# Attention beside a gated MLP on one core: shifted keys by SBUF copies, zero products in TensorE's pauses

## Chip, core and metric

The kernel runs on one core of a Trainium2 chip. The metric is the device time of one launch in microseconds (us), lower is better. The engines are named as in the profile: PE is TensorE (matrix products; PEld is its weight load), ACT is ScalarE, DVE is VectorE, POOL is GpSimd, SP is SyncE, which here only issues DMAs.

## What is computed

Two blocks read the same x (2048 rows, 512 columns), and a sigmoid gate mixes their outputs row by row. Block A is attention with 32 query heads of width 16 over one shared key and value head. Block B is a gated MLP whose gate goes through a 2048 x 2048 product along the sequence.

```python
# S = 2048, D = 512, H = 32, Dh = 16, Fh = 688; bfloat16
g = sigmoid((x * gate_w).sum(-1, keepdims=True))
q = (x @ wq).reshape(S, H, Dh);  k = x @ wk;  v = x @ wv        # one key/value head
p = softmax(q_h @ k.T * Dh ** -0.5);  a = concat_h(p @ v) @ wo
z = gelu(x @ w_in);  z1, z2 = z[:, :Fh], layernorm(z[:, Fh:])
b = (z1 * (w_sp @ z2 + b_sp[:, None])) @ w_out
out = g * a + (1 - g) * b
```

## The kernel before

All data stay in SBUF. The queries, keys and values lie transposed, with heads along partitions. x is loaded by four transposing DMAs, one for each chunk of 512 rows; the chunks come in the order `XO = (0, 3, 2, 1)`.

**Units and blocks.** Attention runs in `NU = 32` units. Unit u takes chunk u // 8 of the queries and four heads. Its scores are 64 blocks: 16 key tiles of 128 rows (`NKT`), times four heads `g` that lie in four partition groups of 32. A block is a product of 32 partitions, 128 keys x 512 queries (`s_mm`, name ps<-QA,KA). The blocks of a unit go two ways. Most are read from PSUM by ACT, which takes the exponential (`exp_op`, P<-ps, two or three blocks in one instruction). The others, up to `NMAX = 8` batches of four blocks a unit, are approximated by a polynomial on DVE: a linear step out of PSUM (`d_A`, UW<-ps), a square (`d_u`) and a second square (`d_w`, UW<-UW), of which POOL takes a part. PE then multiplies all results with the values (ps<-P,V; ps<-UW,V; ps<-UW,VW) and adds two closing products per unit (ps<-QA,KTV and ps<-CT,SVB), whose operands POOL prepares in the head. A unit's products with the values begin when those of the unit before are through.

**Two halves of the keys.** A head has 16 values, a partition group 32. One query tile `QA` thus holds two units: unit 2i uses the lower 16 partitions of each group, unit 2i + 1 the upper 16. `KA[:, 0, :]` holds the keys in the lower halves with zeros above, `KA[:, 1, :]` the shifted keys, in the upper halves with zeros below. Each is a product of x with a weight tile that has zero columns in the other half: `wk_r[0]` is `wk_rep`, `wk_r[1]` lies in the last 512 columns of `z1f` (names xT,wk_rep and xT,z). `g_K(c, lo, hi, e)` makes the products of a chunk, four pieces of four products, and DVE casts them out of PSUM (L426, KA<-ps).

**The planner.** The order of the instructions is planned when the kernel is built. `pe_step`, `act_step` and `dve_step` simulate PE, ACT and DVE with constant durations; each takes the next ready work when it is free, and the instructions are emitted into each engine's queue in that order. On the chip a queue runs strictly in order and waits on semaphores, whatever the plan thought. Constants steer the choice: `A_OV` is the overhead of one ACT instruction in ns, `FLEX` the backlog of DVE (ns) under which the PSUM bank 4, which both can use, goes to DVE instead of to a third block for ACT, `N0 = 3` the batches that unit 0 may give to DVE. `T[key]` is the planned time at which something is ready; the weights `win` have a constant there, 28000 ns. At most `ND = 5` batches are open at once, and a batch of unit u needs the last chunk of that unit's keys (`("K1", 3)` for an odd unit).

**The head.** `WARM` products of constants run before the first x is there. The list `first` holds, in order, the keys, first queries and values of the four chunks, then the shifted keys of the four chunks. Where PE finds no work and was busy for less than `W_MIN` (0.9) of the last `W_WIN` (3400 ns), `pe_step` emits a zero product (ps<-CT,zer, four products into a free bank), but only after 20 us of planned time.

**SP's queue** holds the x transposes, a query weight load, then `ld_win` and `ld_rest` (the bias row, `wo` in eight DMAs, `wout`, the first transposed `w_sp`). These later loads are chained: each waits until the one before has landed (`sp_dma`).

**The end.** After the last unit DVE normalises, and four products each finish the last four tiles of 128 rows (`g_out(14)`, `g_out(15)`, `g_fin(12)`, `g_fin(13)`). Tiles 14 and 15 leave PSUM through ACT (`outsb<-ps,G`), the former is stored by SP's queue, the latter by ACT's.

Of the kernel before, what the change touches and what calls it, by code (L numbers as in the profile page):

```python
# [7 lines left out]
ALU = mybir.AluOpType  # L8
# [8 lines left out]
DH = 16  # L17
# [4 lines left out]
NU = 32  # L22
# [18 lines left out]
NZ = 22  # L41
WARM = 12
RLAST = 16
XO = (0, 3, 2, 1)
N0 = 3
A_OV = 63.3
HEAD = 45000.0
# [8 lines left out]
W_GEL = 0.98  # L56
PR = dict(HALF=100.0, IDR=10, IDN=4, WRES=16, D_HG=2500.0, D_FL=False, WIN=1000.0, WIH=560.0, BACK=32, PRESS=5, FLEX=5000.0, RMIN=32, WBL=0.5, W_MIN=0.9, HOLD=0.0, RLEND=0)
SCHED = {}
# [108 lines left out]
def build_kernel(nc, x_d, wq_d, wk_d, wv_d, wo_d, win_d, wsp_d, bsp_d, wout_d, gw_d, out_d):  # L167
    es = ExitStack()
    with es:
# [75 lines left out]
        SF = tmp[:, 64 * NMAX:96 * NMAX].rearrange("p (k w) -> p k w", w=32)  # L245
        wk_r = [wk_rep[:], z1f[:, 512 * NZ - 512:512 * NZ].rearrange("p (a n) -> p a n", a=4)]
        PT = z2[:, 0:2048].bitcast(F32).rearrange("p (a n) -> p a n", a=2)
# [6 lines left out]
        op("dve", lambda v: v.memset(CT[:], 1.0 / 64.0), w=["CT"])  # L254
# [39 lines left out]
        op("act", lambda q: q.dma_start(wvg[:, :, 0:DH], wv_d.rearrange("(dt p) d -> p dt d", p=128)), w=["wv"], dma=16)  # L294
        op("act", nonc(lambda q: q.dma_start(wvg[:, :, 2 * DH:2 * DH + 1], gw_d.rearrange("(dt p one) -> p dt one", p=128, one=1))), w=["gw"], dma=16)
        def ld_win():
            sp_dma(lambda q: q.dma_start(win[:], win_d.rearrange("(dt p) n -> p dt n", p=128)), w=["win"])
# [28 lines left out]
        for e in range(2):  # L326
            op("dve", lambda v, e=e: v.tensor_scalar(wk_r[e].rearrange("p a (g e d) -> p a g e d", e=2, d=DH)[:, :, :, e, :],
                                                     wk_sb[:].unsqueeze(2).broadcast_to([128, 4, 4, DH]), 0.25, None, ALU.mult),
               r=["wk"], w=[("wk_rep", e)])

# [30 lines left out]

        ld_win()
        ld_rest()
        for _ in range(WARM):
# [53 lines left out]

        def g_K(c, lo=0, hi=512, e=0, b=BM):
            key = "K0a" if c == XO[0] and lo == 0 and e == 0 else ("K%d" % e, c)  # L420

            def piece(dt):
                return lambda: fm(b, hi - lo, 0, wk_r[e][:, dt, :], xT[:, dt, 512 * c + lo:512 * c + hi], dt == 0, dt == 3, [("wk_rep", e), ("x", c), ("z1", 5)], "K")

            def ev():
                op("dve", lambda v: v.tensor_copy(KA[:, e, 512 * c + lo:512 * c + hi], bank(b, hi - lo)), r=[bkey(b)], w=[key], tag="Kev")  # L426
# [469 lines left out]
        for i, c in enumerate(XO):  # L896
# [240 lines left out]
        def pv_emit(pu, rnd, t_end):  # L1137
            for g, it in rnd:
                pv_items[pu][g].remove(it)
                pv_done[pu] += 1  # L1140
                pv_g[pu][g] += 1
                it[1](st_["ua"] > pu and pv_g[pu][g] == unit_total(pu) // 4)
                if it[3] is not None:
                    kind, ix = it[3]
                    if kind == "P":
                        pbusy_[ix] = False
                        pfree_[ix] = t_end + 250.0
                    else:
# [87 lines left out]
        pbusy = deque()  # L1236
        pidle = [0]

        def pe_step(now):
            r = pe_work(now)  # L1240
            if r is None:
# [470 lines left out]
        if INFO is not None:  # L1712
            print({"end": last_end, "busy": busy, "batches": len(batches), "hist": hist, "left": left, "sbuf": nc.sbuf_bytes_remaining})
            print("warm", pidle[0])
            INFO.update(T=T, units=units, estart=estart, stepb=stepb, busy=busy, log=log)
        if INFO is not None and st_["pu"] < NU:
# [177 lines left out]
```

## Time and profile before

| | us |
|---|---|
| three runs, median | 729.7 |
| lowest and highest | 729.62 and 729.8 |
| profiled execution, device time | 732.05 |
| its span, first to last instruction | 730.2 |

In the profile a row of a group gives the line, the engine, the operation, the output and inputs by the program's names, the shape and the count, then the busy time and the mean duration, then the idle time just before and what ended it. A row of a timeline gives the start in us, the length in us, the engine, line and names, and in brackets the idle time before. A row of windows gives each engine's busy time in a stretch and at its end the granted PE clock as a share of full speed, the DMA engines' busy share and GB/s. A row of one tile's instructions gives the shortest, median and longest duration in ns and the first and last start in us. DMA rows give the size of one and the median time from issue to landing.

### The profile page before, as it was taken

What the parts mean: (1) busy time and instruction counts of PE and PEld (TensorE: products, weight loads), DVE (VectorE), ACT (ScalarE), POOL (GpSimd) and SP (SyncE); (2) the same over time, 40 slices, a digit from 0 to 9 for tenths busy, and PEclk for the clock granted to TensorE, in tenths of its full rate; (3) what the DMA queues carried; (4) which work ended last, traced back from release to release, by engine and by line L of the source; (5) the groups of instructions that cost most, each with busy time, mean ns of one, the idle gap of its engine ahead of it and who ended that gap; (6) DMA issues with size and microseconds to landing.
All of it is one profiled execution on the core that took longest, in us unless ns stands there. A gap on an engine that the chain in (4) does not pass through costs nothing.

```text
span 730.2 us, 21786 instructions
## 1 busy us (share of the span) xinstructions
PE 714.8 (98%) x9037; PEld 208.4 (29%) x9037; DVE 704.5 (96%) x1035; ACT 711.9 (98%) x760; POOL 466.9 (64%) x437
## 2 busy tenths in 40 slices
PE   8999999999999999999999999999999999999996
PEld 3322333323422223222222222222232222222321
DVE  5799999999999999999999999999999999999995
ACT  4999999999999999999999999999999999999996
POOL 5643666662166778776677777767776567667661
PEclk8999999999999999999999999999999999999999
DMA  8340000000000000500000051000005100000000
GB/s 189 110 108 10 2 1 2 2 3 2 2 2 1 2 2 2 116 24 9 1 2 2 3 103 36 10 2 1 3 2 105 27 10 9 1 3 2 2 2 33
DMA packets 48608, 17.28 MB, mean 24 GB/s; under 512 B 44180, under 2 KB 47992, under 8 KB 48504
## 3 DMA queue, kind: packets, MB, share of 16 engines
q1 hardware_dynamic: 46248, 15.54, 9.4%
q8 instruction: 72, 1.18, 0.6%
q10 hardware_dynamic: 2256, 0.30, 0.3%
q14 instruction: 32, 0.26, 0.1%
HBM read 3.25 MB, written 2.10 MB: 7 GB/s over the span
## 4 chain that ended last, share of the span: by engine, by line
PE 69%; ACT 17%; DVE 9%; issue 5%; ACTq 0%; DVEq 0%
PE ps L354 69%; ACT P L770 15%; DVE UW L782 4%; DVE UW L789 1%; DVE UW L795 1%; PE ps L353 1%; ACT z L1327 1%; DVE z L584 1%; DVE bst L598 0%; ACT z L592 0%; DVE T L807 0%; DVE km L453 0%; DVE KA L426 0%; DVE QA L471 0%; ACT outsb L728 0%
## 5 line engine op out<-in xcount | busy, mean ns | idle before, releaser
L770 ACT ACTIVATE P<-ps 128x1024 bf16<-128x1024 f32 (+1 forms) x741 | 686.6, 1177 | 7.8 <-PE ps L354 7.5
L795 POOL TENSOR_TENSOR UW<-UW 128x512 f16<-128x512 f16 (+1 forms) x281 | 363.5, 1294 | 161.2 <-DVE UW L795 67.4
L782 DVE TENSOR_SCALAR UW<-ps 128x512 f16<-128x512 f32 (+1 forms) x424 | 347.0, 840 | 4.1 <-PE ps L354 3.1
L354 PE MATMUL ps<-QA,KA 32*128 32x512 bf16 x2048 | 312.8, 386 | 6.1 <-ACT P L770 2.9
L354 PE MATMUL ps<-P,V 128*32 128x512 bf16 x1496 | 212.9, 387 | 0.3 <-DVE KN L499 0.2
L354 PEld LDWEIGHTS ps<-QA,KA 32*128 32x128 bf16 x2048 | 84.5, 91 | 309.7 <-ACT P L770 152.8
L789 DVE TENSOR_TENSOR UW<-UW 128x2048 f16<-128x2048 f16 (+1 forms) x163 | 171.8, 1056 | 0.6
L354 PE MATMUL ps<-UW,VW 128*32 128x512 f16 x552 | 118.9, 384 | 0.0
L354 PE MATMUL ps<-wT,z 128*32 128x512 bf16 (+1 forms) x1536 | 116.2, 366 | 0.0
L795 DVE TENSOR_TENSOR UW<-UW 128x1024 f16<-128x1024 f16 (+5 forms) x167 | 108.4, 664 | 0.2
L354 PE MATMUL ps<-UW,V 128*32 128x512 f16 x552 | 84.4, 384 | 0.2 <-DVE T L807 0.2
L354 PEld LDWEIGHTS ps<-P,V 128*32 128x32 bf16 x1496 | 49.0, 94 | 57.0 <-issue 51.1
L475 POOL TENSOR_TENSOR QSQ<-QA 128x512 bf16<-128x512 bf16 x16 | 28.9, 1806 | 22.9 <-DVE z L612 7.0
L354 PEld LDWEIGHTS ps<-wT,z 128*32 128x32 bf16 x1536 | 27.7, 94 | 42.5 <-issue 41.9
L354 PEld LDWEIGHTS ps<-UW,VW 128*32 128x32 bf16 x552 | 28.1, 94 | 15.0 <-issue 11.6
L354 PE MATMUL ps<-wout,z 128*32 128x512 bf16 x384 | 31.6, 384 | 0.0
L354 PE MATMUL ps<-win,xT 128*32 128x344 bf16 x512 | 30.8, 312 | 0.1
L830 POOL TENSOR_TENSOR Tn<-T,rc 128x512 bf16<-128x512 f32 x15 | 24.6, 1638 | 6.4 <-DVE UW L782 3.1
L807 DVE STREAM_TRANSPOSE T<-ps 128x512 f32<-128x512 f32 (+1 forms) x33 | 22.7, 691 | 4.1 <-PE ps L354 4.1
L354 PE MATMUL ps<-QA,KTV 128*32 128x512 bf16 x128 | 25.0, 384 | 0.0
L354 PE MATMUL ps<-CT,SVB 128*32 128x512 bf16 x128 | 24.6, 384 | 0.0
L354 PEld LDWEIGHTS ps<-UW,V 128*32 128x32 bf16 x552 | 20.0, 94 | 15.6 <-issue 11.3
(116 smaller groups left out, 380.1 us busy)
## 6 DMA issues: line engine op xcount, KB each, us to landing
out_dram<-outsb SPq DMA_DIRECT2D x15, 128.0 KB, 1.7
win<-in_B_w_in_dram SPq DMA_DIRECT2D x1, 1376.0 KB, 6.0
wout<-in_B_w_out_dram SPq DMA_DIRECT2D x1, 640.0 KB, 4.8
wo<-in_A_wo_dram SPq DMA_DIRECT2D x8, 64.0 KB, 2.3
UW<-in_A_wq_dram SPq DMA_DIRECT2D x1, 384.0 KB, 4.0
wT<-in_B_w_sp_dram SPq DMA_TRANSPOSE x16, 4.6
UW<-in_A_wq_dram ACTq DMA_DIRECT2D x1, 128.0 KB, 3.9
out_dram<-outsb ACTq DMA_DIRECT2D x1, 128.0 KB, 2.7
```

Source lines behind the costliest of these rows:

```text
L353: return t.matmul(dst, lhsT, rhs, start=start, stop=stop)
L354: return t.matmul(dst, lhsT, rhs, start=start, stop=stop, tile_position=tp)
L475: dq(pl_q, 1050.0, lambda: op("pool", lambda v: v.tensor_tensor(QSQ[:, q % 2, :], QA[:, q % NQ, :], QA[:, q % NQ, :], ALU.mult), r=[("Q", ...
L584: ev = lambda: op("dve", lambda v: v.tensor_copy(z2[:, FH * st + 344 * h:FH * st + 344 * h + 344], bank(BM, 344)), r=[bkey(BM)], w=[("z2", ...
L770: op("act", lambda a: a.activation(P[:, 512 * p0:512 * (p0 + n)], ps[:, 512 * b0:512 * (b0 + n)], ACT.Exp), r=[bkey(b0 + i_) for i_ in ran ...
L782: op("dve", lambda v: v.tensor_scalar(UW[:, 0, s, 512 * i:512 * (i + n)], bank(b, 512 * n), Q_A, Q_AS, ALU.mult, ALU.add), r=[bkey(b + j) ...
L789: op("dve", lambda v: v.tensor_tensor(src, src, src, ALU.mult), r=k, w=k, tag="dTT")
L795: op(eng, lambda v: v.tensor_tensor(UW[:, 1, s, 256 * a:256 * b], src, src, ALU.mult), r=[("U", s, h) for h in range(a // 2, (b + 1) // 2) ...
L807: return lambda: pgx.op("dve", lambda v: v.transpose(T1[:, jj, c0:c1], bank(BO, c1 - c0, c0)), r=[bkey(BO)], w=[("T1", jj, c0)], tag="T1")
L830: pgx.op(eng, lambda v: v.tensor_tensor(tnv[:, pr, j0:j1, b0:b1, :], t1v[:, j0:j1, b0:b1, 0:16], rc[:, j0:j1, b0:b1].unsqueeze(3).broadcas ...
L1327: op("act", lambda a: a.activation(z1f[:, 512 * i0:512 * (i0 + n)], ps[:, 512 * b0:512 * (b0 + n)], ACT.Gelu_apprx_tanh), r=[bkey(b0 + j) ...
```

## The change

The shifted keys are no longer products. When a chunk of keys is cast, SP issues four DMAs (`ld_K1`), one for each partition group, that copy 16 partitions of `KA[:, 0]` to the 16 above in `KA[:, 1]`; POOL sets `KA[:, 1]` to zero at the start. The second weight tile and its preparation on DVE go. The later loads are issued between these copies, behind the cast of a chunk: `win` behind the copies of chunks 3 and 0, the bias row and `wo` behind chunk 2's, the rest behind chunk 1's. Zero products are allowed in the head from `W_HEAD` = 9000 ns on, in any pause (threshold 1.0 until 20 us), and after the last product with the values for `W_TAIL` = 1850 ns, into bank 1. One of the twelve warm-up products goes. The stores of tiles 14 and 15 change queues. `A_OV` and `FLEX` get new values.

```diff
-WARM = 12
+WARM = 11
+W_HEAD = 9000.0
+W_TAIL = 1850.0
-A_OV = 63.3
+A_OV = 62.9
-PR = dict(... FLEX=5000.0 ...)
+PR = dict(... FLEX=4000.0 ...)
...
-        for e in range(2):
-            op("dve", lambda v, e=e: v.memset(wk_r[e], 0.0), w=[("wk_rep", e)])
+        op("dve", lambda v: v.memset(wk_rep[:], 0.0), w=["wk_rep"])
...
+        op("pool", lambda g: g.memset(KA[:, 1, :], 0.0), w=[("K1", c) for c in range(4)])
...
+        spc = {"free": 13200.0}
+
+        def ld_K1(c, t):
+            def issue(q):
+                return [q.dma_start(KA[32 * g + 16:32 * g + 32, 1, 512 * c:512 * c + 512], KA[32 * g:32 * g + 16, 0, 512 * c:512 * c + 512]) for g in range(4)]
+            op("sp", issue, r=[("K0", c)] + (["K0a"] if c == XO[0] else []), w=[("K1", c)], dma=64, tag="K1")
+            spc["free"] = max(spc["free"], t) + 1800.0
+            T[("K1", c)] = spc["free"] + 2200.0
...
         def ld_rest():
-            ld_bsp(0)
-            sp_dma(ld_wo, w=["wo"], n=128)
...
-        ld_win()
-        ld_rest()
         for _ in range(WARM):
...
             def done(t):
                 T[key] = t
-                if e == 0 and all(("K0", c2) in T for c2 in range(4)) and hi == 512:
+                if hi == 512 and c == XO[1]:
+                    ld_K1(c, t)
+                    ld_K1(XO[0], t)
+                    ld_win()
+                elif hi == 512 and c == XO[2]:
+                    ld_K1(c, t)
+                    ld_bsp(0)
+                    sp_dma(ld_wo, w=["wo"], n=128)
+                elif hi == 512 and c == XO[3]:
+                    ld_K1(c, t)
+                    ld_rest()
+                if all(("K0", c2) in T for c2 in range(4)) and hi == 512:
...
-                       g_K(XO[3]), g_V(XO[3])] + [g_K(c, e=1) for c in (XO[1], XO[0], XO[2], XO[3])])
+                       g_K(XO[3]), g_V(XO[3])])
...
-                       g_out(14, BM, None, True, "sp"),
-                       g_out(15, DBK[0], lambda: d_done(), True, "act"),
+                       g_out(14, BM, None, True, "act"),
+                       g_out(15, DBK[0], lambda: d_done(), True, "sp"),
...
+                if st_["pu"] == NU:
+                    tend[0] = t_end
...
-                if now > 20000.0 and b < (W_GEL if gst["arm"] and gst["t"] > now - 8000.0 else pr["W_MIN"]) * W_WIN:
+                if u >= NU and tend[0] is not None and now + C_V <= tend[0] + W_TAIL:
+                    fm(EB[1][0] + 1, 512, 0, zer[:], CT[:], True, True, ["zer", "CT"], "warm")
+                    pidle[0] += 1
+                    r = now + C_V
+                elif now > W_HEAD and b < (1.0 if now < 20000.0 else W_GEL if gst["arm"] and gst["t"] > now - 8000.0 else pr["W_MIN"]) * W_WIN:
```

More of the change, by code (lines that the diff above doesn't have):

```diff
@@ L56 @@
 W_GEL = 0.98
-PR = dict(HALF=100.0, IDR=10, IDN=4, WRES=16, D_HG=2500.0, D_FL=False, WIN=1000.0, WIH=560.0, BACK=32, PRESS=5, FLEX=5000.0, RMIN=32, WBL=0.5, W_MIN=0.9, HOLD=0.0, RLEND=0)
+PR = dict(HALF=100.0, IDR=10, IDN=4, WRES=16, D_HG=2500.0, D_FL=False, WIN=1000.0, WIH=560.0, BACK=32, PRESS=5, FLEX=4000.0, RMIN=32, WBL=0.5, W_MIN=0.9, HOLD=0.0, RLEND=0)
 SCHED = {}
@@ L245, in build_kernel @@
         SF = tmp[:, 64 * NMAX:96 * NMAX].rearrange("p (k w) -> p k w", w=32)
-        wk_r = [wk_rep[:], z1f[:, 512 * NZ - 512:512 * NZ].rearrange("p (a n) -> p a n", a=4)]
         PT = z2[:, 0:2048].bitcast(F32).rearrange("p (a n) -> p a n", a=2)
@@ L324, in ld_rest @@
             ld_wT(0)
[L326 to L329, printed above, removed]
+        op("dve", lambda v: v.tensor_scalar(wk_rep[:].rearrange("p a (g e d) -> p a g e d", e=2, d=DH)[:, :, :, 0, :],
+                                            wk_sb[:].unsqueeze(2).broadcast_to([128, 4, 4, DH]), 0.25, None, ALU.mult),
+           r=["wk"], w=["wk_rep"])
         def wq_tile(eng, t, key, raw):
@@ L417, in qt, with g_K @@
             return 1e12 if t is None else t
-        def g_K(c, lo=0, hi=512, e=0, b=BM):
-            key = "K0a" if c == XO[0] and lo == 0 and e == 0 else ("K%d" % e, c)
+        def g_K(c, lo=0, hi=512, b=BM):
+            key = "K0a" if c == XO[0] and lo == 0 else ("K0", c)
             def piece(dt):
-                return lambda: fm(b, hi - lo, 0, wk_r[e][:, dt, :], xT[:, dt, 512 * c + lo:512 * c + hi], dt == 0, dt == 3, [("wk_rep", e), ("x", c), ("z1", 5)], "K")
+                return lambda: fm(b, hi - lo, 0, wk_rep[:, dt, :], xT[:, dt, 512 * c + lo:512 * c + hi], dt == 0, dt == 3, ["wk_rep", ("x", c)], "K")
             def ev():
-                op("dve", lambda v: v.tensor_copy(KA[:, e, 512 * c + lo:512 * c + hi], bank(b, hi - lo)), r=[bkey(b)], w=[key], tag="Kev")
+                op("dve", lambda v: v.tensor_copy(KA[:, 0, 512 * c + lo:512 * c + hi], bank(b, hi - lo)), r=[bkey(b)], w=[key], tag="Kev")
             def done(t):
                 T[key] = t
-                if e == 0 and all(("K0", c2) in T for c2 in range(4)) and hi == 512:
+                if hi == 512 and c == XO[1]:
[10 more added lines that the diff above has]
+                if all(("K0", c2) in T for c2 in range(4)) and hi == 512:
                     for c2 in range(4):
@@ L1237, in build_kernel @@
         pidle = [0]
+        tend = [None]
         def pe_step(now):
@@ L1714, in build_kernel @@
             print("warm", pidle[0])
-            INFO.update(T=T, units=units, estart=estart, stepb=stepb, busy=busy, log=log)
+            INFO.update(pg=pg, T=T, units=units, estart=estart, stepb=stepb, busy=busy, log=log)
         if INFO is not None and st_["pu"] < NU:
```

## The prediction

> **What bounds the kernel now.** I read the page first: the busy shares, then the slices, then the groups.
>
> ```profile
> span 730.2 us, 21786 instructions
> PE 714.8 (98%) x9037; PEld 208.4 (29%) x9037; DVE 704.5 (96%) x1035; ACT 711.9 (98%) x760; POOL 466.9 (64%) x437
> ACT  4999999999999999999999999999999999999996
> PEclk8999999999999999999999999999999999999999
> L770 ACT ACTIVATE P<-ps 128x1024 bf16<-128x1024 f32 (+1 forms) x741 | 686.6, 1177 | 7.8 <-PE ps L354 7.5
> L782 DVE TENSOR_SCALAR UW<-ps 128x512 f16<-128x512 f32 (+1 forms) x424 | 347.0, 840 | 4.1 <-PE ps L354 3.1
> L354 PE MATMUL ps<-P,V 128*32 128x512 bf16 x1496 | 212.9, 387 | 0.3 <-DVE KN L499 0.2
> L789 DVE TENSOR_TENSOR UW<-UW 128x2048 f16<-128x2048 f16 (+1 forms) x163 | 171.8, 1056 | 0.6
> L795 DVE TENSOR_TENSOR UW<-UW 128x1024 f16<-128x1024 f16 (+5 forms) x167 | 108.4, 664 | 0.2
> L354 PE MATMUL ps<-UW,V 128*32 128x512 f16 x552 | 84.4, 384 | 0.2 <-DVE T L807 0.2
> ```
>
> ACT, PE and DVE are all full from the second slice to the last: nothing inside the long run can be removed by this change. 1496 blocks of scores take the exponential on ACT and 552 a polynomial on DVE, and the planner shifts blocks between the two. So time given to either engine anywhere is shared by both. A block costs ACT 686.6 / 1496 = 0.459 us and DVE (347.0 + 171.8 + 108.4) / 552 = 1.136 us. If ACT gains a and DVE gains d, the end moves by (a / 0.459 + d / 1.136) / (1 / 0.459 + 1 / 1.136) = 0.71 a + 0.29 d. That is the exchange rate of everything below.
>
> Second, the stretches of the head, where PEclk is below 9 and the engines do wait.
>
> ```profile
> core 0: us, PE busy (x) PEld busy (x) DVE busy (x) ACT busy (x) POOL busy (x), PEclk, DMA share, GB/s
> 10.40:13.90 3.50, 2.49 (x85) 1.19 (x84) 1.45 (x6) 3.44 (x4) 3.14 (x7) 1.00 1.13 176
> 13.90:20.80 6.90, 6.90 (x77) 1.26 (x78) 4.51 (x7) 5.16 (x7) 2.41 (x6) 0.51 0.65 215
> 20.80:30.00 9.20, 9.13 (x277) 3.94 (x265) 7.39 (x16) 9.20 (x10) 6.91 (x12) 1.00 0.27 65
> 30.00:34.60 4.60, 4.59 (x61) 1.29 (x56) 2.46 (x6) 4.60 (x6) 3.88 (x11) 1.00 0.42 146
> 11.25 0.39 PE L354 MATMUL ps<-QA,KA 32*128 32x512 bf16 x3 [0.79 <-ACT P L770]
> 33.26 0.69 DVE L782 TENSOR_SCALAR UW<-ps 128x512 f16<-128x512 f32 x1 [1.02 <-PE ps L354]
> ```
>
> PE pauses for 1.01 us of 10.4 to 13.9 (the longest pause 0.79 us), and at 13.9 the granted clock falls to 0.51 for 6.9 us. In those 6.9 us PE is full, ACT waits 6.90 - 5.16 = 1.74 us and DVE 2.39 us. From 20.8 to 34.6 ACT waits no more, but DVE idles 1.81 + 2.14 = 3.95 us, for score products (the 1.02 us wait is one). Unit 0 gives DVE three batches at most, and for unit 1 it needs the shifted keys, which come later still (next part).
>
> **The products removed.**
>
> ```profile
> L354 PE MATMUL ps<-xT,z x64: 379/389/392, 29.9 to 40.6; 128*32 128x512 bf16 x64
> L426 DVE CAST KA<-ps x9: 292/692/693, 7.5 to 42.1; 128x512 bf16<-128x512 f32 x7, 128x128 bf16<-128x128 f32 x1, 128x384 bf16<-128x384 f32 x1
> 29.91 0.64 PE L354 MATMUL ps<-xT,z 128*32 128x512 bf16 x8
> L354 PE MATMUL ps<-CT,zer x148: 379/379/390, 23.1 to 563.1; 128*32 128x512 bf16 x148
> ```
>
> The 64 products on the second weight tile go, 16 groups of four; two groups last 0.64 us with the latency of the end, so a group takes about 0.22 and all of them 3.5 us of PE. With them go four of the nine casts: 4 x 0.692 = 2.77 us of DVE. PE is not what the sum goes by: it gets 3.5 us here and up to 3.4 from the clock (half of 6.9), more than the two others.
>
> **The copies added.** Sixteen DMAs from SBUF to SBUF, four for each chunk of keys, 16 KB each. The trace of before has no such copy.
>
> ```profile
> 6.37 6.05 SPq L287 DMA_TRANSPOSE xT<-in_A_x_dram x2
> 12.10 0.69 DVE L426 CAST KA<-ps 128x512 bf16<-128x512 f32 x1 [1.94 <-PE ps L354]
> 14.63 0.38 SPq L297 DMA_DIRECT2D win<-in_B_w_in_dram x1
> 22.00 4.70 SPq L306 DMA_DIRECT2D wo<-in_A_wo_dram x8
> wo<-in_A_wo_dram SPq DMA_DIRECT2D x8, 64.0 KB, 2.3
> win<-in_B_w_in_dram SPq DMA_DIRECT2D x1, 1376.0 KB, 6.0
> 9.79 2.71 POOL L333 COPY wqd<-UW 128x256 bf16<-128x256 bf16 x6 [5.03 <-DMA UW<-in_A_wq_dram]
> 37.06 0.39 PE L354 MATMUL ps<-QA,KTV 128*32 128x512 bf16 x2
> ```
>
> The nearest row is the eight loads of wo: 4.70 / 8 = 0.59 us to issue one, 2.3 us to land. SP is free of the transposes at 12.4 and the first cast it waits for ends at 12.8. So the copies of chunk 3 are issued by 12.8 + 4 x 0.59 = 15.2 and land by 17.5, those of chunk 0 by 19.9. Behind them on SP wait win, the bias row, wo and the rest. win is issued at about 17.5 instead of 14.6; the plan starts its products at 28.0 by a constant that the change leaves, and here its load needs 6 us, so it is in by 23.5. The copies of chunk 1 stand behind the load of win, the bias row and the eight issues of wo, and land near 34. Unit 0's 52 blocks keep ACT, which is at work by 10.4, for 23.9 us, and the 16 blocks of chunk 0 come first in unit 1, 7.3 us: chunk 1 is wanted near 41 (unit 0's closing products start at 37.06). I cost the copies at nothing. The cover for chunk 3 is unit 0's own three DVE batches, 12 x 1.136 = 13.6 us that can't begin before 12.8, so until 26; if the copies landed some 9 us later it would be gone, and PE would stand still for the difference with ACT's and DVE's score products queued behind, since it takes its queue in order. The added clearing of the second key half on POOL is covered by POOL's wait of 5.03 us ahead of 9.79.
>
> What it gives: DVE can go on to unit 1 as soon as unit 0's batches are through. All the idle time from 13.9 to 34.6 is 2.39 + 3.95 = 6.34 us, with the casts 9.1 us. Ends: 2.77 (only the casts) and 9.1. DVE waits for PE's score products in nearly all of it and PE stays full, so I take half of the idle time: d = 2.77 + 3.2 = 5.9 us, worth 0.29 x 5.9 = 1.7 us.
>
> **Zero products in the head.** From 9 to 20 us the planner now fills every pause of PE that it sees. If the clock then stays whole, the 1.74 us come back to ACT: 0.71 x 1.74 = 1.2 us. Lower end: the pause of 0.79 us is one that PE spends behind a score product that waits for ACT, in program order; a plan that doesn't see it can't fill it.
>
> The Trainium skill (TensorE: Matmul & The Clock Gate, "Why this matters for your kernels") says that the clock stays up as long as no pause is longer than about 3 us, and its Part 1 that one busy window of 3.4 us brings it back. The trace differs on both: the pause was 0.79 us, and PE was full for 6.9 us before the clock rose. By that rule the zero products would change nothing and this term would be 0.
>
> **One warm-up product less.**
>
> ```profile
> 1.44 5.30 PE L353 MATMUL ps<-CT 128*128 128x512 bf16 x12 [1.44 <-DVE CT L254]
> 6.67 0.59 PE L354 MATMUL ps<-xT,wk_rep 128*32 128x128 bf16 x16
> DMA to landing us min/median/max: 5.1/5.7/6.7
> ```
>
> The twelve take 5.30 us, 0.43 each. The first key product follows at once; the x transposes land 5.1 us after issue at the soonest and open SP's queue, so the first can be in at about 6. Between 0 (x or the clock later than that) and 0.43; I take 0.25, as PE then meets more of its half clock: 0.71 x 0.25 = 0.2 us.
>
> **The end.**
>
> ```profile
> 721.86 0.39 PE L354 MATMUL ps<-P,V 128*32 128x512 bf16 x2
> 724.32 1.05 PE L354 MATMUL ps<-wo,OT 128*32 128x512 bf16 x16 [2.07 <-DVE OT L838]
> 725.21 0.69 ACT L728 ACTIVATE outsb<-ps,G 128x512 bf16<-128x512 f32 x1 [3.40 <-PE ps L354]
> 725.93 0.37 ACTq L662 DMA_DIRECT2D out_dram<-outsb  x1
> 726.40 0.69 ACT L728 ACTIVATE outsb<-ps,G 128x512 bf16<-128x512 f32 x1 [0.50 <-ACT outsb L728]
> out_dram<-outsb SPq DMA_DIRECT2D x15, 128.0 KB, 1.7
> out_dram<-outsb ACTq DMA_DIRECT2D x1, 128.0 KB, 2.7
> ```
>
> The last sixteen products come after 2.07 us without work and take 1.05 us, 0.22 a group and the latency: already whole speed. Zero products for 1.85 us of that wait speed up nothing here; they end before 724.32, so they cost nothing either. The swap of the last two stores does act. ACT now issues a store between its two last activations and the second starts 0.50 us late; with the other one on its queue that goes. But the last store then lands by ACT's queue, 2.7 us in its one row against 1.7 on SP's. Ends 0 and 0.5; I take 0.2.
>
> **The sum.** 1.7 + 1.2 + 0.2 + 0.2 = 3.3 us. The profiled execution took 732.05 us (its span 730.2 and 1.85 around it): 728.7 after. The runs' median is 729.7, 2.35 below that execution; the same 3.3 us off gives **726.4 us**. The two constants A_OV (63.3 to 62.9 ns, 0.3 us over 741 activations) and FLEX I set at nothing here; FLEX has a rival below.
>
> With every upper end the gain is 0.71 x 2.17 + 0.29 x 9.1 + 0.5 = 4.7 us, 725.0. With only the casts, half of the clock's loss and nothing at the end it is 0.29 x 2.77 + 0.71 x 0.87 = 1.4 us, 728.3.
>
> **Rivals.** *The clock falls in the head all the same.* For it: the pause that the planner doesn't see. Against it: with the zero products the window holds more work. The skill's rule above, too, would leave the fall where it is. Then ACT gets 0.25 us, DVE its casts and half of the 3.95 us after 20.8: 0.71 x 0.25 + 0.29 x 4.75 + 0.2 = 1.8 us, 727.9.
>
> *Freed time stays unused.* DVE's idle time is put down to PE throughout, and PE stays full; the clock's gain goes into PE's own backlog. Then the casts, the earlier start and the end are left: 0.8 + 0.2 + 0.2 = 1.2 us, 728.5, within the bound below.
>
> *DVE is starved in the long run.* FLEX falls from 5000 to 4000: the PSUM bank that ACT's larger steps and DVE share goes to DVE only when its backlog is below 4 us. Now DVE idles 4.1 us ahead of 424 of these instructions, so there is no slack to lose. The gain is gone when DVE idles 3.3 / 0.29 = 11 us more, 1.6% of its time. With 24 waits of 0.7 us (the head's in the row above is 1.02) it is 17 us: 4.9 - 3.3 = 1.6 us slower, 731.3. Against it: a block that DVE doesn't get goes to ACT in a step of three, which is ACT's better step.
>
> **How the numbers follow.** Forecast 0.55, clock falls 0.17, unused 0.13, starved 0.15. The measurement can tell about 0.2%, 1.5 us, from no change: 728.2 and 731.2. Faster: nearly all of the forecast, somewhat over half of the second, a third of the third, in all 0.69; within the bound 0.15; slower 0.16, from the starved case and a plan whose last units happen to end badly. The likeliest case's own range is 725.0 to 728.3; a closing batch more or less on DVE (4 x 1.136 = 4.5 us of one engine, 0.29 of it the end) adds 1 us on the low side; the high side reaches into the starved case: 724.2 to 731.2.
>
> **What would show it.** Right: no casts of shifted keys, the granted clock near 1 through 13.9 to 20.8, ACT busy there near 6.9, DVE near full from 26, the second last activation straight behind the first. Wrong: a half clock at some place of the head or later, PE waiting for a key copy, long waits of DVE ahead of the polynomial's first step (L782 now), or ACT's busy time per block above 0.459 us.

## The result, and the profile after

The change made the kernel slower. Six executions after it gave a median of 732.72 us (732.09 to 735.22), six of the kernel before on the same chip 729.66 us (729.55 to 729.97): a ratio of 1.0041, interval 1.003 to 1.0051. The forecast was 726.4 us, with a range of 724.2 to 731.2. The profiled execution after took 735.22 us, the slowest of the six, with a mean granted clock of 0.992; the three executions at 0.997 took 732.1 to 732.4.

The page of the kernel after: the span, PE's and the clock's slices, ACT's exponential, DVE's first polynomial step, and the products that count ACT's blocks (1492, so DVE has 556 of the 2048, four more than before).

```profile
span 733.4 us, 21844 instructions
PE 715.0 (98%) x9052; PEld 208.4 (28%) x9052; DVE 705.6 (96%) x1040; ACT 710.9 (97%) x760; POOL 472.5 (64%) x438
PEclk9899999999999999999999999999999999999999
L786 ACT ACTIVATE P<-ps 128x1024 bf16<-128x1024 f32 (+1 forms) x741 | 685.7, 1170 | 11.3 <-PE ps L361 10.9
L798 DVE TENSOR_SCALAR UW<-ps 128x512 f16<-128x512 f32 (+1 forms) x424 | 348.0, 842 | 6.2 <-PE ps L361 5.5
L361 PE MATMUL ps<-P,V 128*32 128x512 bf16 x1492 | 211.5, 388 | 0.1
```

DVE took a batch of blocks more and ACT's busy time fell (711.9 to 710.9), yet ACT waits 11.3 us ahead of its exponentials instead of 7.8. In this execution the time is lost in waits, and the windows say where: the stretches that the prediction used, and the next one.

```profile
10.40:13.90 3.50, 2.07 (x75) 0.93 (x67) 0.69 (x1) 3.05 (x4) 3.11 (x7) 1.00 1.17 172
13.90:20.80 6.90, 6.64 (x60) 1.47 (x61) 3.66 (x8) 4.52 (x4) 2.96 (x7) 0.57 0.31 64
20.80:30.00 9.20, 9.20 (x200) 2.97 (x197) 7.34 (x14) 7.68 (x9) 4.52 (x11) 0.77 0.56 183
30.00:34.60 4.60, 4.60 (x116) 1.74 (x109) 4.60 (x8) 4.60 (x8) 4.06 (x7) 1.00 0.34 81
34.60:42.10 7.50, 6.01 (x74) 1.82 (x68) 7.47 (x10) 6.46 (x8) 6.77 (x11) 1.00 0.34 105
```

The third column is DVE, the fourth ACT, the clock stands after POOL. From 13.9 to 20.8 the clock is again at half (0.57), ACT does 4.52 us of work instead of 5.16, and the fall goes on into the next stretch (0.77), where before had none. DVE is full from 30 on. From 34.6 to 42.1 PE stands still for 1.49 us and ACT for 1.04; before both are full there (7.50 of 7.50). The half clock belongs to this execution: another one with the same plan, shown below, does not have it in these stretches.

### The profile page after: what moved, and what is told of

It is laid out like the page before. It is cut to its first block, busy times and chain, and to the rows that moved or that the text cites. A ratio compares the mean times of both kernels' runs of the same rounds, so it can differ in the third digit from the quotient of the medians.

```text
span 733.4 us, 21844 instructions
## 1 busy us (share of the span) xinstructions
PE 715.0 (98%) x9052; PEld 208.4 (28%) x9052; DVE 705.6 (96%) x1040; ACT 710.9 (97%) x760; POOL 472.5 (64%) x438
## 4 chain that ended last, share of the span: by engine, by line
PE 70%; ACT 13%; DVE 11%; issue 5%; DMA 1%; ACTq 0%; DVEq 0%
PE ps L361 70%; ACT P L786 12%; DVE UW L798 5%; DVE UW L805 3%; DVE UW L811 2%; DMA xT<-in_A_x_dram 1%; ACT z L1350 1%; DVE bst L614 0%; DVE T L823 0%; ACT z L608 0%; DVE QA L487 0%; DVE km L469 0%; DVE outsb L746 0%; ACT L608 0%; DVE OT L854 0%
## 5 line engine op out<-in xcount | busy, mean ns | idle before, releaser
L786 ACT ACTIVATE P<-ps 128x1024 bf16<-128x1024 f32 (+1 forms) x741 | 685.7, 1170 | 11.3 <-PE ps L361 10.9
L811 POOL TENSOR_TENSOR UW<-UW 128x512 f16<-128x512 f16 (+1 forms) x281 | 368.7, 1312 | 165.9 <-DVE UW L811 63.3
L805 DVE TENSOR_TENSOR UW<-UW 128x2048 f16<-128x2048 f16 (+1 forms) x171 | 175.4, 1027 | 0.8
L361 PE MATMUL ps<-UW,VW 128*32 128x512 f16 x556 | 121.7, 384 | 0.0
L491 POOL TENSOR_TENSOR QSQ<-QA 128x512 bf16<-128x512 bf16 x16 | 26.7, 1670 | 18.5 <-DVE UW L798 9.3
L846 POOL TENSOR_TENSOR Tn<-T,rc 128x512 bf16<-128x512 f32 x15 | 21.5, 1435 | 8.5 <-DVE UW L811 3.0
L361 PE MATMUL ps<-CT,SVB 128*32 128x512 bf16 x128 | 22.6, 384 | 0.0
L361 PE MATMUL ps<-xT,win 128*32 128x512 bf16 (+1 forms) x384 | 22.5, 363 | 0.0
```

The lines of the kernel that those rows point to most:

```text
L361: return t.matmul(dst, lhsT, rhs, start=start, stop=stop, tile_position=tp)
L491: dq(pl_q, 1050.0, lambda: op("pool", lambda v: v.tensor_tensor(QSQ[:, q % 2, :], QA[:, q % NQ, :], QA[:, q % NQ, :], ALU.mult), r=[("Q", ...
L786: op("act", lambda a: a.activation(P[:, 512 * p0:512 * (p0 + n)], ps[:, 512 * b0:512 * (b0 + n)], ACT.Exp), r=[bkey(b0 + i_) for i_ in ran ...
L805: op("dve", lambda v: v.tensor_tensor(src, src, src, ALU.mult), r=k, w=k, tag="dTT")
L811: op(eng, lambda v: v.tensor_tensor(UW[:, 1, s, 256 * a:256 * b], src, src, ALU.mult), r=[("U", s, h) for h in range(a // 2, (b + 1) // 2) ...
L846: pgx.op(eng, lambda v: v.tensor_tensor(tnv[:, pr, j0:j1, b0:b1, :], t1v[:, j0:j1, b0:b1, 0:16], rc[:, j0:j1, b0:b1].unsqueeze(3).broadcas ...
```

## The experiments

### The kernel before, again, and each part alone

*The kernel before, unchanged.*

> The kernel before, unchanged, to see how often its clock falls in the head. If the fall in the profiled execution (13.9 to 20.8) is what made it 732.05 against a median of 729.7, its timed executions have a mean clock near 0.997 instead of 0.993 and lie at 729.7, and most executions have no fall. If the fall is usual and costs nothing, they have 0.993 at 729.7.

Measured: 729.95 us (729.48 to 730.99, 12 executions), beside 730.06 in the 29 of the same chip, ratio 0.9989 [0.9978, 0.9999]. The profiled one of the twelve took 730.99 us, the slowest of them, but it has no fall of the clock in the head. Its windows aren't what the prediction read:

```profile
10.40:13.90 3.50, 2.74 (x84) 1.18 (x84) 1.75 (x6) 3.44 (x5) 3.13 (x7) 1.00 1.14 171
13.90:20.80 6.90, 6.50 (x132) 2.18 (x130) 6.56 (x14) 6.90 (x9) 3.98 (x9) 1.00 0.76 239
20.80:30.00 9.20, 9.20 (x227) 3.72 (x231) 6.09 (x12) 9.20 (x11) 7.76 (x18) 1.00 0.24 62
30.00:34.60 4.60, 4.60 (x61) 1.28 (x57) 3.85 (x7) 4.60 (x5) 3.97 (x10) 1.00 0.47 151
```

Same program, same longest pause (0.79 us), clock 1.00 in all four stretches, ACT full from 13.9. Of the 29 executions seven lie at 731.97 to 732.49 with a mean clock of 0.993, that of the execution profiled first; the other 22 lie at 729.5 to 730.5 with 0.995 to 0.998. So the fall, if the same mean clock stands for the same fall, costs some 2.2 us and isn't in the median. It was in the one that was profiled. It came in seven of these 29 executions, but in none of the twelve; of all 136 timed executions of this kernel on five chips 17 have a clock of 0.993, one in eight.

*The two constants alone.*

```diff
-A_OV = 63.3    FLEX=5000.0
+A_OV = 62.9    FLEX=4000.0
```

> The kernel before with A_OV 62.9 and FLEX 4000 alone. Theory that the constants matter for the whole run (DVE starved, or another order of all later work): 731 to 733. Theory that they only shift details: 729.7 within 0.7.

Measured: 731.47 us (730.95 to 733.68, 12), ratio 1.0019 [1.0008, 1.0029]. Two numbers of the planner, set at nothing in the sum, cost 1.4 us. The last part of this section returns to them.

*The copies and the loads between alone* (from the kernel after):

```diff
-WARM = 11, W_HEAD = 9000.0, W_TAIL = 1850.0, A_OV = 62.9, FLEX=4000.0
+WARM = 12, W_HEAD = 20000.0, W_TAIL = 0.0, A_OV = 63.3, FLEX=5000.0
-g_out(14, ..., "act"), g_out(15, ..., "sp")
+g_out(14, ..., "sp"), g_out(15, ..., "act")
```

> The kernel before with the copies alone (and the later loads between them): twelve warm-up products, no zero products in head or end, stores and constants as before. Forecast's theory: DVE and ACT get their share of 3.5 us of PE and 2.77 us of DVE, 728 or less. Rival: the freed time meets other waits of the head (POOL's chain, the loads), no change, 729.7 within 0.7. Rival that the copies are late: 731 or more, with PE waiting for a key copy.

Measured: 731.95 us (731.24 to 734.18, 12), ratio 1.0024 [1.0013, 1.0035]. A second look at it:

> Placeholder of the copies-alone kernel for one look at its profile again beside the others: 731 to 732.5, PE waiting for DVE's polynomial between 25 and 50.

Its one execution took 732.34 us, within the twelve. So the copies as they stand lose 1.9 us.

*The zero products of head and end alone* (in the kernel before):

```diff
+W_HEAD = 9000.0, W_TAIL = 1850.0
-if now > 20000.0 and b < (...) * W_WIN:
+if u >= NU and ... now + C_V <= tend[0] + W_TAIL: ...
+elif now > W_HEAD and b < (1.0 if now < 20000.0 else ...) * W_WIN:
```

> The kernel before with the zero products of head and end alone. Theory that the zero products hurt the head (they use up PE's instructions and stand in front of real products): 731.5 to 734, PE standing still without a wait near 12.5. Theory that they are harmless: 729.7 within 1, and no fall of the clock in the head in any execution.

Measured: 736.76 us (735.8 to 738.14, 6), ratio 1.008 [1.0065, 1.0094], the slowest of all and beyond the 734 expected, at mean clocks of 0.996 to 0.999. PE's timeline in the head, of this kernel, of the kernel after, of the kernel after with its last two stores on their old queues (its experiment follows below; the plan is the same), then of the unchanged kernel (start, length, work; in brackets the idle time before it and what ended it):

```profile
8.99 1.25 PE L356 MATMUL ps<-CT,zer 128*32 128x512 bf16 x20
11.80 0.68 PE L356 MATMUL ps<-wvg,xT 128*32 128x33 bf16 x53
14.16 0.25 PE L356 MATMUL ps<-wvg,xT 128*32 128x33 bf16 x11 [1.67 <-issue]
```
```profile
9.05 1.25 PE L361 MATMUL ps<-CT,zer 128*32 128x512 bf16 x20
11.86 0.61 PE L361 MATMUL ps<-wvg,xT 128*32 128x33 bf16 x54
14.02 0.24 PE L361 MATMUL ps<-wvg,xT 128*32 128x33 bf16 x10 [1.54 <-issue]
```
```profile
13.90 0.24 PE L361 MATMUL ps<-wvg,xT 128*32 128x33 bf16 x10 [1.27 <-issue]
```
```profile
12.05 0.66 PE L354 MATMUL ps<-wvg,xT 128*32 128x33 bf16 x64
```

With twenty zero products ahead of it, the group of 64 small value products breaks after 53 or 54, and PE stands still for 1.20 to 1.67 us with "issue" as the releaser: it waits for nothing that the profile shows. Without them the 64 run through. Counted from PE's first instruction, the break comes after 222 pairs of weight load and product in all four profiles that have the zero products in the head (this one has a warm-up product more and one of the 64 fewer ahead of the break; the fourth is the kernel after without POOL's chain, below, 1.20 us). That the engine ran out of fetched instructions fits, but no run varied it alone. The standstill is longer than the pause that the zero products were to fill (0.79 us). It does not decide on the clock: the four kernels have the same break, and from 13.9 to 20.8 their clock is 0.75 (this one), 0.57 (the kernel after), 1.00 and 1.00. Two windows of the third, which runs the plan of the kernel after:

```profile
13.90:20.80 6.90, 6.76 (x143) 2.40 (x143) 5.20 (x13) 6.23 (x7) 3.04 (x8) 1.00 0.28 60
34.60:42.10 7.50, 6.36 (x54) 1.48 (x56) 5.93 (x8) 4.91 (x5) 6.26 (x18) 0.66 0.30 98
```

Its clock falls only later, to a mean of 0.66 from 34.6 to 42.1.

### The kernel after with one part back

*Without zero products in the head.*

```diff
-W_HEAD = 9000.0
+W_HEAD = 20000.0
```

> The changed kernel with zero products in the head only after 20 us, as before; copies, constants, stores and the zero products of the end stay. Theory: the 24 zero products of 9 to 15 us make PE run out of instructions (it stands for 1.5 us after its 222nd product, at 12.5, in both kernels that have them) and push the first DVE batch back; without them no standstill, and the first 21 us hold some 30 blocks instead of 21. Then 731 to 732, what is left being the copies' and the constants'. Rival that the zero products are worth their price in the changed kernel (they keep the clock up): slower than 732.7, with falls of the clock in more executions.

Measured: 733.95 us (733.34 to 735.67, 5), ratio 1.0055 [1.0039, 1.0071], slower than the 731 to 732 expected. The interval overlaps the kernel after's (1.003 to 1.0051), so the zero products of the head show neither a gain nor a loss in this kernel. Nor is it the rival's clock: four of the five executions have 0.998 or 0.999. The standstill was gone and 30 blocks were done by 21 us, as in the unchanged kernel, but by 50 us they were 106 against 109. Its head is that of the copies alone, with the same two slow steps of DVE (1.90 us at 41.23, 1.52 us at 43.05) that a later part takes up. What it loses beyond the copies alone isn't traced.

*With the last two stores on their old queues*, the plan being the same:

```diff
-g_out(14, ..., "act"), g_out(15, ..., "sp")
+g_out(14, ..., "sp"), g_out(15, ..., "act")
```

> The changed kernel with the last two stores on their old queues; the plan is the same to the instruction. Theory: the last store lands later from ACT's queue (the span ended 8.3 us after the last product with the values, 7.9 before), so this is 0.3 to 0.5 us faster than the changed kernel, 732.3. Rival (the forecast's term): 0.2 to 0.5 us slower, 733.

Measured: 732.13 us (731.02 to 734.54, 12), ratio 1.0026 [1.0015, 1.0036]: its median is 0.6 us under the kernel after, but the two intervals overlap. The end of the kernel after:

```profile
727.12 1.05 PE L361 MATMUL ps<-wo,OT 128*32 128x512 bf16 x16 [0.34 <-DVE OT L854]
728.00 1.26 ACT L744 ACTIVATE outsb<-ps,G 128x512 bf16<-128x512 f32 x2 [3.64 <-PE ps L361]
728.35 2.84 SPq L678 DMA_DIRECT2D out_dram<-outsb  x3
729.29 0.37 ACTq L678 DMA_DIRECT2D out_dram<-outsb  x1
```

The two activations now follow each other directly, as forecast. But ACT's store goes out only behind both of them, 2.17 us after the last products begin (1.60 with the old queues), and from there to the end of the span it is 733.4 - 727.12 = 6.28 us; with the old queues 730.7 - 724.78 = 5.92. This difference is within the scatter: the kernel before has 5.88 us in one profiled execution and 729.1 - 721.88 = 7.22 in the other. So no run shows the gain that was forecast, and the loss isn't clear either. The sixteen last products take 1.05 us with and without zero products ahead of them.

### POOL's chain left out

In the head POOL works through a queue: running sums for unit 1's closing values, then sixteen small copies of the gate (`RT`), and behind these the squared keys and queries (`KSQ`, `QSQ`). These three kernels leave the sums and the sixteen copies out and set the gate's tile to a constant.

```diff
-for i in range(NMAX - 2, -1, -1): op("pool", ... SF ..., ALU.add)
-for i in range(NMAX - 2, -1, -1): op("pool", ... KF ..., ALU.add)
-for g in range(4): for k in range(4): op("pool", ... tensor_copy(RT ..., E ...))
+op("pool", lambda g: g.memset(RT[:], 0.5), w=["RT"])
```

> The copies alone, same plan, but POOL's work of the head is left out: the running sums of the closing operands and the sixteen small copies of the gate (a constant stands in the gate's place; the output is another). Theory: with the copies DVE is full from 21 us, just while POOL runs that chain; DVE's squares are stretched (2.5 us between 20 and 50), PE and ACT wait for DVE, and it is never made up. Without POOL's work the squares take their usual time and it is 1.5 to 2.5 us faster than with it: 729.5 to 730.5. Rival: DVE is simply given more than it can do, whatever POOL does: 731.9, no change.

> Control: the kernel before with the same work of POOL left out. Theory: DVE has 3.9 us of idle time between 21 and 40 there and makes the stretching up, so nothing changes: 729.9 within 0.5. If POOL's chain costs as much here, about 728, and the copies aren't what brings the two together.

> The changed kernel with the same work of POOL left out. Theory: the same stretching (1.7 us), and besides PE's standstill of 1.5 us at 34 to 39 for the squared keys, which POOL makes late, goes: 2.5 to 4 us faster than the changed kernel, 729 to 730; the standstill after the 222nd product at 12.5 stays. Rival: the loss lies in the zero products of the head and in the clock, 732 or more.

Measured: the copies alone 729.77 us (729.23 to 731.91, 11), ratio 0.9996 [0.9986, 1.0006]; the kernel before 730.14 (729.24 to 731.03, 11), 1.0000 [0.9991, 1.0009]; the kernel after 730.52 (730.02 to 732.03, 11), 1.0008 [0.9999, 1.0017]. POOL's chain costs the kernel before nothing and the other two about 2.2 us each (2.1 and 2.5 against the kernel before beside each run), with intervals that lie apart. The last one stayed above the 729 to 730 expected. The two kernels with the copies alone run the same plan, so their timelines can be laid side by side. With POOL's chain (windows of 40.7 to 44.2 and 44.2 to 50, then DVE, POOL, PE and ACT):

```profile
40.70:44.20 3.50, 2.94 (x29) 0.64 (x27) 3.50 (x4) 3.08 (x4) 2.12 (x2) 1.00 0.16 39
44.20:50.00 5.80, 5.07 (x57) 1.35 (x57) 5.80 (x8) 4.92 (x6) 0.56 (x1) 1.00 0.72 145
40.81 1.90 DVE L805 TENSOR_TENSOR UW<-UW 128x2048 f16<-128x2048 f16 x1
42.64 1.52 DVE L811 TENSOR_TENSOR UW<-UW 128x1024 f16<-128x1024 f16 x1
32.76 6.58 POOL L583 COPY RT<-E 32x16 f32<-32x16 f32 x16
40.59 1.04 POOL L491 TENSOR_TENSOR QSQ<-QA 128x512 bf16<-128x512 bf16 x1
42.43 1.19 POOL L453 TENSOR_TENSOR KSQ<-KA 128x512 bf16<-128x512 bf16 x1 [0.79 <-PE ps L361]
42.77 0.39 PE L361 MATMUL ps<-UW,V 128*32 128x512 f16 x1 [0.37 <-DVE UW L805]
43.55 1.02 ACT L786 ACTIVATE P<-ps 128x1024 bf16<-128x1024 f32 x1 [0.42 <-PE ps L361]
```

Without it:

```profile
40.70:44.20 3.50, 3.46 (x42) 0.89 (x40) 3.50 (x6) 3.50 (x5) 1.07 (x1) 1.00 0.05 15
44.20:50.00 5.80, 5.45 (x70) 1.66 (x66) 5.80 (x9) 5.80 (x7) 2.12 (x2) 1.00 0.45 93
40.72 1.20 DVE L798 TENSOR_TENSOR UW<-UW 128x2048 f16<-128x2048 f16 x1
41.85 0.68 DVE L804 TENSOR_TENSOR UW<-UW 128x1024 f16<-128x1024 f16 x1
38.72 1.04 POOL L492 TENSOR_TENSOR QSQ<-QA 128x512 bf16<-128x512 bf16 x1 [9.87 <-DVE UW L804]
38.37 8.43 ACT L779 ACTIVATE P<-ps 128x1024 bf16<-128x1024 f32 x9
```

The same two polynomial steps take 1.90 and 1.52 us where POOL runs a squaring beside them, and 1.20 and 0.68 where it doesn't. DVE is full, so its 1.54 us come out of the end of its chain; PE, which takes its queue in order, stops for DVE (0.37 us at 42.77), and ACT, full until then, stops for PE (0.42 us at 43.55; from 40.7 to 50 ACT works 8.00 of 9.30 us). By 50 us it has finished 106 blocks of exponentials and polynomials, the other 110; by 400 us 1081 and 1088. In these two executions the gap closes at 425 to 450, where the clock fell for a while in the one without POOL's chain (the windows' clock there is 0.93, against 1.00), and their spans differ by 0.3 us only; the 2.2 us are the medians' of 12 and 11 executions. The sixteen small copies don't stretch anything themselves: the two steps that run wholly beside them, at 35.35 and 38.04, keep 1.21 and 0.67 us. They hold POOL until 39.3, and so two squarings fall on the polynomial steps. Without the chain the squarings still run, at 38.72 and 42.35, and stretch no step. Whether the sums or the sixteen copies make them late wasn't separated. The unchanged kernel in the same place:

```profile
34.60:42.10 7.50, 7.50 (x87) 1.99 (x85) 7.50 (x9) 7.50 (x10) 4.71 (x12) 1.00 0.35 81
38.97 1.04 POOL L437 TENSOR_TENSOR KSQ<-KA 128x512 bf16<-128x512 bf16 x1
38.47 1.21 DVE L782 TENSOR_SCALAR UW<-ps 128x1024 f16<-128x1024 f32 x1
45.40 1.04 POOL L437 TENSOR_TENSOR KSQ<-KA 128x512 bf16<-128x512 bf16 x1 [5.39 <-PE ps L354]
45.99 1.53 DVE L789 TENSOR_TENSOR UW<-UW 128x2048 f16<-128x2048 f16 x1
```

There the copies hold POOL just as long (until 38.9), and DVE is as full (the third column, 7.50 of 7.50 us). But the first squaring stands beside a step out of PSUM, which keeps its 1.21 us, and the next one costs 0.32 us. Over 20 to 50 us the squares of the polynomial take 0.4 us more than their usual time in the unchanged kernel, 2.5 us with the copies, and 0.8 us with the copies less POOL's chain. So what the copies change is which steps of DVE the squarings meet; that DVE's idle time ahead of it (up to 34 us) covers for POOL in the kernel before, no run shows by itself.

The Trainium skill (SBUF — State Buffer, "SBUF: two separate sides") says that a DVE instruction with two inputs in SBUF and a POOL instruction that reads SBUF share one pair of ports as an exclusive lock, the second one blocked until the first is done. The rows agree: the first step ends at 42.71, 1.08 us after POOL's squaring (40.59 + 1.04), the second at 44.16, 0.54 us after the squaring that ends at 43.62. Each is its usual time of 1.20 and 0.68 us less some 0.13, as if it had begun only when the squaring was done. The step at 45.99 in the unchanged kernel ends 1.08 us after its squaring too. The sixteen small copies read SBUF as well and show nothing of it.

The kernel after meets it in another form. There PE itself waits for a squaring:

```profile
39.53 0.40 PE L361 MATMUL ps<-KSQ,quar 128*32 128x512 bf16 x4 [1.49 <-POOL KSQ L453]
31.21 3.97 POOL L571 TENSOR_TENSOR z<-z 128x64 f32<-128x64 f32 x7
35.25 3.11 POOL L573 CAST KTV<-z 32x512 bf16<-32x512 f32 x4
38.44 1.04 POOL L453 TENSOR_TENSOR KSQ<-KA 128x512 bf16<-128x512 bf16 x1
38.59 1.96 DVE L805 TENSOR_TENSOR UW<-UW 128x2048 f16<-128x2048 f16 x1
```

POOL comes to the squaring only at 38.44, behind the sums and the casts. A step of DVE is stretched beside it (1.96 us), and this is PE's standstill of 34.6 to 42.1 in the windows above. The six executions of the kernel after had a mean clock of 0.992 to 0.997, the eleven without POOL's chain 0.997 to 1.000: part of its 2.2 us may be the clock's, which wasn't separated.

### The constants, in pairs

Is the gain of the copies there at all, and what does a constant do by itself? Each pair has the kernel before with a new A_OV alone, and the copies less POOL's chain with the same A_OV.

```diff
-A_OV = 63.3
+A_OV = 62.7   (or 63.1, or 63.5)
```

> The kernel before with A_OV 63.1 in place of 63.3. Theory that before's own constants are a good draw: 731 to 733, with nothing else changed. Rival: 730 within 0.5.

> The kernel before with A_OV 63.5. Theory of the draw: 731 to 734. Rival: 730 within 0.5.

> The copies with POOL's chain left out, with A_OV 63.5: to stand against the kernel before at the same constant (leaving the chain out changed nothing for that kernel). Theory: at a constant that isn't tuned for either, the copies gain the 2 to 3 us that the products cost, 729.5 to 731 against 732 to 734. Rival (the copies gain nothing even so): within 0.7 of the kernel before at 63.5.

> The copies alone with A_OV 63.1, POOL's running sums and the gate's 16 copies left out (so the output is another; POOL's chain alone is what is left out). The kernel before with the same constant took 733.46. Theory, that the copies themselves are worth about 1 us once POOL's chain doesn't stretch DVE's squares, and that the rest is the draw of the plan: 731 to 733, under 733.46. Rival, that the new constant costs the same kind of loss whatever the copies do, and the copies are worth nothing: 733 to 734. A time below 730.5 would say that what a constant does to one kernel says nothing of what it does to another.

> The kernel before with A_OV 62.7 alone. The values tried so far gave 729.7 to 730.1 at 63.3, 731.47 at 62.9 with FLEX 4000, 733.46 at 63.1, 731.22 at 63.5. Theory, that a constant only redraws the plan and that 63.3 is a good draw: 731 to 733.5. Rival, that the time follows the constant smoothly and falls below 62.9: under 730.5.

> The copies alone with A_OV 62.7 and POOL's chain left out as above (the output is another), the pair of the run with A_OV 62.7 alone. Theory, copies worth about 1 us at equal constants, with a draw beside it: 0 to 3 us under its pair. Rival, copies worth nothing: within 0.7 us of its pair on either side, or slower.

| A_OV | before, us | copies less POOL's chain, us | difference |
|---|---|---|---|
| 62.7 | 732.04 (6) | 729.88 (10) | -2.16 |
| 63.1 | 733.46 (4) | 731.16 (7) | -2.30 |
| 63.3 | 729.97 (33) | 729.77 (11) | -0.20 |
| 63.5 | 731.22 (10) | 730.24 (10) | -0.98 |

In brackets are the executions. The copies lie under their pair all four times, by 1.4 us in the mean; by the intervals against the kernel before, only the pair at 62.7 stands clear by itself (1.0033 [1.002, 1.0045] and 1.0002 [0.9989, 1.0014]). That POOL's chain costs the kernel before nothing is measured at 63.3 alone, so at the other values part of the difference could be POOL's chain in the kernel before. A mark of the copies is in the count of ACT's blocks, here at 62.7 for the kernel before and for the copies:

```profile
L354 PE MATMUL ps<-P,V 128*32 128x512 bf16 x1500 | 212.5, 385 | 0.1
L362 PE MATMUL ps<-P,V 128*32 128x512 bf16 x1492 | 205.6, 385 | 0.1
```

DVE takes two batches of four blocks more at 62.7, one more at each other value (1500 and 1496 at 63.1; 1496 and 1492 at 63.3 and 63.5).

The first column says something else: all other values of the constant tried on the kernel before (62.9 with FLEX 4000 among them) cost it 1.2 to 3.5 us, with no order in them. A constant of the planner can move every later decision a little; these times fit a plan that comes out as a draw. The kernel before holds a good one, 2.1 us under the mean of the other four.

### Two versions meant to be better

The gate's copies go to POOL four at a time, between other work, instead of sixteen in a row; the first kernel with A_OV 63.5, the second with 62.6 and FLEX 3500.

```diff
-for k in range(4): op("pool", ... RT ...)
+def rt(g=g): ...four copies...
+dq(pl_q, 4 * 400.0, rt, t, setT("RT") if g == 3 else None)
```

> A version meant to be better: the copies alone, with the gate's sixteen copies handed out four at a time at moments that the planner chooses (as it does with POOL's other later work) instead of at once, and A_OV 63.5. Theory: less stretching between 33 and 40, 730 to 731; if the sums before it stretch DVE as much, 731.5 or more.

> The version with the copies and the gate's sixteen POOL copies handed out by the planner (730.5 at A_OV 63.5, FLEX 5000), with A_OV 62.6 and FLEX 3500. Theory that the two constants redraw the whole plan by a microsecond or two: 728 to 730.5, faster than both kernels if the draw is good. Rival that the constants are harmless: 730.5 within 0.4.

Measured: 730.52 us (729.91 to 732.5, 11), ratio 1.0009 [1.0000, 1.0018]; and 729.56 us (729.1 to 731.43, 11), ratio 0.9994 [0.9984, 1.0003]. Neither leaves anything out. The first lies 0.7 us under the kernel before at the same A_OV (731.22), with intervals that overlap; in its profile no square between 34 and 50 us is stretched. The second is the fastest whole kernel that was found, 0.5 us under the kernel before beside it (730.05). Its interval holds 1, so it is level.

## Why the prediction was wrong

**The clock's term (1.2 us): the step that failed first.** The fall at 13.9 was read rightly. It was priced at 1.2 us by ACT's wait alone and costs some 2.2 us, but in an execution that has it, and most have none. The prediction saw that its execution stood 2.35 us above the median and then took "the same 3.3 us off" the median, from which the clock's term had nothing to take. Nor did the zero products end the falls: of the four profiled executions that have them in the head, two fell there (in that of the kernel after for longer) and two did not. Whether they change how often the clock falls, no run shows. The Trainium skill (TensorE: Matmul & The Clock Gate, Part 1) says that the window in which the clock gate counts runs free, so that one kernel has another number of slow products from run to run. The 29 executions differ in such a way; that the window is the reason, no run here shows.

**The zero products in the head were costed at their gain alone.** The step said that a plan might not see the pause. It saw it, and twenty products more brought a standstill of 1.54 us waiting for nothing that the profile shows. The step did not ask what else they could cost. In the kernel before they cost 6.7 us, at a clock no lower than its own; in the kernel after, taking the head's back gained nothing.

**The copies, costed at nothing.** As DMAs they do cost nothing:

```profile
13.25 5.97 SPq L301 DMA_DIRECT2D KA<-KA  x8
19.27 0.58 SPq L307 DMA_DIRECT2D win<-in_B_w_in_dram  x1
KA<-KA SPq DMA_DIRECT2D x16, 16.0 KB, 2.3
```

The first eight took 0.75 us each instead of the 0.59 forecast, `win` went out at 19.3 instead of 17.5, a landing took 2.3 us as forecast, and no engine is shown waiting for a key copy. The gain d came near too: DVE's idle time from 21 to 40 us went from 3.86 us to 0.03 with the copies alone, with the casts' 2.77 us 6.6 against 5.9 forecast; and the four pairs show 1.4 us in the mean (0.2 to 2.3) against the 1.7 forecast. One reading was off: DVE was said to wait for score products in nearly all of its idle time, but from 13.9 to 34.6 they end 3.0 of 6.3 us, products for keys and values 2.9. What failed is that the step looked at DVE, PE and SP and, past the first 10 us, not at POOL. With the copies two of POOL's squarings fall on DVE's squares (1.54 us of stretching), and POOL's chain costs 2.2 us in all, more than the gain.

**A_OV and FLEX, set at nothing.** The step counted 0.3 us over 741 activations and one rival (a starved DVE). DVE wasn't starved: from 60 us to 720 it waits 1.6 us ahead of the polynomial's first step, 1.2 before. The constants cost 1.4 us alone. A plan that they redraw fits this, as A_OV by itself costs 1.2 to 3.5 us with no order; FLEX wasn't varied by itself. A redraw had no place in the sum or the rivals, only a vague one in the chance of slower.

**The end (+0.2).** No run shows the gain: the second activation starts at once, but the end is 0.4 us longer in the trace and 0.6 in the medians, both within the scatter. Nor was the row of 2.7 us against 1.7 a price of the queue: of the last four stores before the change SP's three took 2.8 us in the median and ACT's 2.7. **The warm-up product (+0.2).** The lower end, 0, held: with eleven and with twelve the first key products wait for x and start at the same time.

```profile
6.36 0.41 PE L361 MATMUL ps<-xT,wk_rep 128*32 128x128 bf16 x16 [0.83 <-DMA xT<-in_A_x_dram]
```

(In the unchanged kernel they start at 6.35.) Two sums of the prediction were slips that change little: 5.30 / 12 is 0.44, and 0.29 x 4.5 us is 1.3, which puts the low end at 723.7. The 24 waits of 0.7 us of its third rival have no row behind them.

The parts don't add up: alone, constants, copies and zero products cost 1.4, 1.9 and 6.7 us, together 3.1. Each changes the plan, so a loss measured for a part can hold its own effect and a draw. Shown with an equal plan is only the cost of POOL's chain, 2.2 us, of which the clock may hold a part in the kernel after; the copies' gain rests on the four pairs. Of the zero products' 6.7 us some 2 lie outside the span: all six executions have 3.5 to 4.0 us around it (738.14 - 734.4 = 3.7 in the profiled one), where nearly all others have 1.8. Why, and how much of the rest is the standstill and how much the draw, stays open.

## What to carry to other kernels

Before a term read from one profiled execution is taken off a median, ask whether the median execution has it: the distance between the two, and the spread of clocks over many executions, is the answer. When work moves earlier on an engine that is almost full, ask which other engine's work it will then stand beside. And where a planner sets the order, a change to any of its inputs is a new draw of the whole plan: compare at several values of a neutral constant before a difference of a few tenths of a per cent is given to the edit.

## What the runs showed of the hardware

The clock fell to half (0.51 from 13.9 to 20.8) with a longest pause of 0.79 us and a total of 1.01 us in 3.5 ahead of it, and stayed at 1.00 in another profiled execution of the same program with the same longest pause; the first one's mean clock, 0.993, came in 17 of 136 executions. PE stood still 1.2 to 1.7 us after exactly 222 pairs of load and product in the four profiled executions in which twenty products more were put into the first 12 us. A DVE step with both inputs in SBUF went from 1.20 to 1.90 us beside one squaring of POOL, while beside small copies of POOL's it kept its 1.21 us.
